# A new order, buffer list and engine list for a fused RWKV-5 and MLP-mixer kernel, with twenty zero products in place of sixteen

## The chip, the core and the metric

The kernel runs on one core of one Trainium2 chip. The metric is the device time of one launch in microseconds (us). Five engines work side by side and wait for one another through semaphores: TensorE (PE in the profile, with its weight loads as PEld), VectorE (DVE), ScalarE (ACT), GpSimd (POOL) and SyncE (SP), which here only issues transfers.

## What is computed

Four sequences of 768 steps and 8 heads of 48 channels go through a linear recurrence with a decaying state, and its output goes through one token-mixing and one channel-mixing MLP with residuals:

```python
for t in range(S):
    cur = np.einsum('bhd,bhe->bhde', u[None] * kt, vt)
    y[:, :, t] = np.einsum('bhd,bhde->bhe', rt, state + cur)
    state = w[None, :, :, None] * state + np.einsum('bhd,bhe->bhde', kt, vt)
...
h = np.maximum(xt @ w_tok1, 0.0) @ w_tok2
u = x + h.transpose(0, 2, 1)
h2 = np.maximum(u @ w_ch1, 0.0) @ w_ch2
return (u + h2)
```

Inputs and output are float32; the products run on bfloat16 copies that accumulate in float32. Nothing of this differs between the two kernels.

## The kernel before

**Tiling.** The recurrence is computed in chunks of 128 steps, six for each of the four batches. In a chunk, k and r are scaled by powers of w (tiles `kr`), turned so that the channels lie on the rows (`tk`, `tr`, `trk` on TensorE, then copied to `ka`, `rka` or `rkb`; from the third batch on by a transposing DMA), multiplied into scores (`at_ps`), masked by VectorE (`AT`), and multiplied with v (`y_ps`). The part that comes from earlier chunks is a product of `rkb` with the state `S`; the state is gathered in a bank `kv_ps` and read out after each chunk. A chunk's own term (u times k times r) is a product of `pr` with `u_blk` (`ad_ps`, then `adg`), multiplied with v by GpSimd (`ydb`) and added into `y_ps`. `y_ps` is read out to `x_b`.

**The first batch** (`pair_unit`, line 823) does two chunks at a time, called window 0, 1 and 2 here: even and odd steps (j = 0, 1) are loaded together (tiles `zr`). For a window TensorE does 8 transposes each of k and r, 32 score products that each use 48 rows and 64 columns of the array, 16 products for `ad_ps`, 16 for `kv_ps` and 32 for `y_ps` that use 64 rows, and some more; an `x N` of the profile often covers half a window. The score products come in two groups of 16 for each window.

**The MLP** of a batch (`mixer`, line 1010) follows when its x is there: `h_ps<-x_b`, `hx_ps` or `hT_ps`, then 12 groups of three `z_ps` products for each half, whose relu is `zr` (written by ScalarE or VectorE), then the `h_ps<-wch,zr` products, the sum to `osb` and the store.

**Order.** Nothing in it is left to a scheduler. `Plan.add` (line 216) collects 886 tasks (890 after the change), each with what it depends on, and `Plan.run` (line 230) emits them in the order of the table `ORDER`. Every engine call goes through `InOrder` (line 273), so each engine's queue has that order, and all rows of the profile name its line 279. `BUFS` gives the buffer number of each tile as it is taken (`m` are the seven PSUM banks), and `ENGINES` says for each task that has a choice which of two engines does it (`flex`, line 223).

**Zero products.** `keep_warm` (line 1191) multiplies a tile of zeros with itself into a bank of PSUM. A wide one is one product of 512 columns; one in quarters is four products of 128 columns each, into the last 128 columns, which the state does not use. `NWARM` is their number and `WIDE_AT` lists the wide ones; a wide one must stand ahead of the first state product of the bank, one in quarters may stand anywhere in the table.

```python
for i in range(512 // cols):
    pe.matmul(bank[0][:, 512 - cols:512], warm[:, 0:128], warm[:, 0:cols], start=fresh or cols == 512, stop=True,
              skip_group_check=True)
```

**Two products with one row.** `w_ps` and `u_ps` (the `spread` function; line 496 for `u_ps`) copy a row of w or u to all partitions: one float32 product of a single row with 384 columns each, which the profile shows as two records.

Of the kernel before, what the change touches and what calls it, by code (L numbers as in the profile page):

```python
# [66 lines left out]
    0, 1, 2, 0, 1, 0, 2, 0, 1, 2, 0, 1, 2, 1, 0, 1, 2, 1, 0, 1, 2, 0, 1, 2,  # L67
],
    'AT1': [
    0, 1, 2, 0, 1, 0, 2, 0, 1, 0, 2, 0, 1, 2, 0, 1, 2, 1, 0, 2, 1, 0, 2, 1,  # L70
# [11 lines left out]
    0, 1, 2, 3, 4, 0, 1, 3, 2, 4, 0, 1, 3, 4, 2, 0, 1, 3,  # L82
# [11 lines left out]
    0, 1, 2, 3, 4, 5, 0, 3, 1, 2, 5, 4, 0, 3, 2, 5, 0, 1, 2, 4, 3, 0, 5, 1, 4, 3, 2,  # L94
# [3 lines left out]
    0, 1, 2, 3, 4, 5, 2, 0, 1, 3, 4, 5, 2, 3, 0, 5, 1, 4,  # L98
],
    'ku': [  # L100
    0, 1, 0, 0, 1, 0, 1, 0, 1, 0, 0, 1,
# [13 lines left out]
],  # L115
    'osb': [
    0, 1, 2, 2, 1, 0, 1, 0, 0, 1, 0, 1, 2, 0, 2, 1, 2, 1, 2, 0, 0, 2, 1, 0, 2,
],
    'pr': [
    0, 1, 1, 0, 1, 0,  # L120
# [5 lines left out]
    0, 1, 2, 3, 0, 1, 2, 3, 1, 0, 3, 2,  # L126
],
    'rka': [
    0, 1, 2, 0, 1, 0,
# [6 lines left out]
    0, 1, 0, 1, 0, 1, 1, 0, 1, 1, 0, 1,  # L136
],
    'rt': [
    0, 1, 2, 3, 4, 0, 2, 3, 1, 0, 4, 2,
# [6 lines left out]
    0, 1, 2, 1, 2, 0, 1, 2,  # L146
],
    'vb': [
    0, 1, 2, 3, 4, 0, 1, 2, 3, 0, 4, 2, 3, 1, 0, 2, 4, 1,
# [5 lines left out]
    0, 1, 2, 3, 4, 5, 0, 2, 1, 3, 4, 0, 5, 1, 2, 3, 4, 0,  # L155
# [5 lines left out]
    0, 1, 2, 1, 0, 2, 0, 1, 2, 0, 2, 1, 2, 1, 0, 1, 2, 1,  # L161
],
    'ydb': [
    0, 1, 2, 0, 1, 0,
# [4 lines left out]
}  # L169
ENGINES = [  # L170
# [9 lines left out]
]  # L180
NWARM = 16
WIDE_AT = [
    0, 1, 2, 3, 4, 5, 6, 7, 8, 9, 10, 11, 12,
]
# [1051 lines left out]
```

## Time and profile before

| what | value |
|---|---|
| median of 3 runs | 165.35 us (165.35 to 165.37) |
| profiled execution | 165.22 us |
| its span (first to last instruction) | 163.3 us |
| PE busy | 158.4 us (97%) |
| DVE / ACT / POOL busy | 119.5 / 66.2 / 79.6 us |
| mean granted TensorE clock | 0.958 |
| DMA | 26.90 MB, 165 GB/s on average |

The profiled execution is 1.9 us longer than its span, and 0.13 us under the median. "Busy" counts the time from a product's start to its modelled end, and products overlap, so busy says little of how much the array does. The profile gives the share of the clock that was granted to TensorE, as PEclk in its slices and in a view that adds up any stretches that one asks for. A row of the timeline reads: start, time, engine, line, operation, names, rows*columns of the array, rows x columns of the moving operand, type, count, and in brackets the idle time before it with what ended it.

### The profile page before, as it was taken

What the parts mean: (1) busy time and instruction counts of PE and PEld (TensorE: products, weight loads), DVE (VectorE), ACT (ScalarE), POOL (GpSimd) and SP (SyncE); (2) the same over time, 40 slices, a digit from 0 to 9 for tenths busy, and PEclk for the clock granted to TensorE, in tenths of its full rate; (3) what the DMA queues carried; (4) which work ended last, traced back from release to release, by engine and by line L of the source; (5) the groups of instructions that cost most, each with busy time, mean ns of one, the idle gap of its engine ahead of it and who ended that gap; (6) DMA issues with size and microseconds to landing.
All of it is one profiled execution on the core that took longest, in us unless ns stands there. A gap on an engine that the chain in (4) does not pass through costs nothing.

```text
span 163.3 us, 4001 instructions
## 1 busy us (share of the span) xinstructions
PE 158.4 (97%) x1593; PEld 106.9 (65%) x1593; DVE 119.5 (73%) x239; ACT 66.2 (41%) x149; POOL 79.6 (49%) x101
## 2 busy tenths in 40 slices
PE   6999999999999999999999999999999999999991
PEld 1486775777676767676667766677667566666671
DVE  6589576576598999889849996998898552782432
ACT  3678285544772263167346524245532014211100
POOL 7279475803908262998995778837622000000000
PEclk9998555999999999999999999999999999999999
DMA  4999979999999679999999799999941055020332
GB/s 127 262 261 253 237 142 235 185 227 174 200 207 203 108 164 174 215 219 167 195 209 218 161 182 195 223 212 193 160 102 52 0 120 139 30 100 0 110 131 96
DMA packets 86821, 26.90 MB, mean 165 GB/s; under 512 B 81554, under 2 KB 85908, under 8 KB 86804
## 3 DMA queue, kind: packets, MB, share of 16 engines
q1 hardware_dynamic: 84448, 23.40, 70.9%
q0 software_dynamic: 2160, 3.15, 11.4%
q8 instruction: 12, 0.20, 0.6%
q10 hardware_dynamic: 196, 0.11, 0.2%
q14 instruction: 5, 0.04, 0.1%
HBM read 20.46 MB, written 4.72 MB: 154 GB/s over the span
## 4 chain that ended last, share of the span: by engine, by line
PE 94%; ACT 2%; DVE 1%; issue 0%
PE h_ps L279 35%; PE z_ps L279 29%; PE kv_ps L279 8%; PE y_ps L279 7%; PE at_ps L279 4%; PE hT_ps L279 3%; PE hx_ps L279 3%; PE tr_ps L279 2%; ACT rkb L279 1%; PE w_ps L279 1%; PE trk L279 1%; PE ad_ps L279 1%; PE tk_ps L279 1%; ACT ka L279 1%; ACT vb L279 1%; DVE pr L279 0%
## 5 line engine op out<-in xcount | busy, mean ns | idle before, releaser
L279 PE MATMUL h_ps<-wch,zr 128*128 128x384 bf16 (+1 forms) x300 | 54.0, 319 | 0.0
L279 PE MATMUL z_ps<-uT,wch 128*128 128x384 bf16 x288 | 52.3, 327 | 0.0
L279 ACT ACTIVATE zr<-z_ps 128x384 bf16<-128x384 f32 x61 | 28.1, 491 | 51.6 <-PE z_ps L279 51.5
L279 PEld LDWEIGHTS <-wch 128*128 128x128 bf16 x288 | 31.7, 114 | 13.5
L279 PEld LDWEIGHTS <-zr 128*128 128x128 bf16 x300 | 27.4, 97 | 15.2
L279 DVE TENSOR_SCALAR zr<-z_ps 128x384 bf16<-128x384 f32 x35 | 18.4, 554 | 14.0 <-PE z_ps L279 13.9
L279 DVE TENSOR_TENSOR AT<-at_ps,mask 128x512 bf16<-128x512 f32 x36 | 23.2, 681 | 3.2 <-PE at_ps L279 3.2
L279 POOL TENSOR_TENSOR yd<-vb,adg 128x384 f32<-128x384 bf16 x13 | 10.7, 830 | 17.8 <-ACT vb L279 5.1
L279 PEld LDWEIGHTS <-kr 128*128 128x128 bf16 (+1 forms) x196 | 13.3, 107 | 3.5 <-issue 1.1
L279 POOL TENSOR_TENSOR kr<-kt,wnat 128x384 bf16<-128x384 f32 x13 | 13.3, 1026 | 1.7 <-DMA kt<-in_k_dram 0.9
L279 POOL TENSOR_TENSOR ku<-kt,u_bc 128x384 f32<-128x384 f32 x11 | 12.0, 1088 | 2.3 <-DMA kt<-in_k_dram 1.6
L279 DVE TENSOR_TENSOR osb<-u_sb,h_ps 128x384 f32<-128x384 bf16 (+1 forms) x16 | 8.4, 525 | 4.9 <-PE h_ps L279 4.8
L279 PEld LDWEIGHTS <-wtok 128*128 128x128 bf16 x78 | 7.3, 100 | 5.2 <-issue 1.3
L279 DVE TENSOR_TENSOR x_b<-y_ps,yd 128x384 bf16<-128x384 f32 x18 | 9.6, 552 | 1.4 <-PE y_ps L279 1.2
L279 DVE TENSOR_TENSOR u_sb<-x_b,hT_ps 128x384 bf16<-128x384 bf16 x15 | 7.5, 549 | 4.0 <-PE hT_ps L279 4.0
L279 PE MATMUL h_ps<-x_b,wtok 128*128 128x384 bf16 x48 | 9.4, 342 | 0.0
L279 POOL TENSOR_TENSOR rku<-ku,rt 128x384 f32<-128x384 f32 x8 | 8.6, 1079 | 1.3 <-DMA rt<-in_r_dram 1.1
L279 POOL TENSOR_TENSOR pr<-rka,rkb 128x512 bf16<-128x512 bf16 x3 | 3.6, 1213 | 11.5 <-DVE rka L279 4.6
L279 PE MATMUL kv_ps<-vb,kr 128*128 128x96 bf16 (+1 forms) x100 | 8.8, 228 | 0.0
L279 PE MATMUL y_ps<-vb,AT 128*128 128x48 bf16 (+1 forms) x240 | 8.8, 191 | 0.0
L279 POOL TENSOR_TENSOR kr<-rt,wp 128x384 bf16<-128x384 f32 x8 | 8.6, 1081 | 0.0
L279 ACT CAST S<-kv_ps 48x192 bf16<-48x192 f32 x20 | 6.3, 313 | 5.2 <-PE kv_ps L279 5.0
(108 smaller groups left out, 211.4 us busy)
## 6 DMA issues: line engine op xcount, KB each, us to landing
out_dram<-osb SPq DMA_DIRECT2D x23, 192.0 KB, 2.2
kt<-in_k_dram SPq DMA_DIRECT2D x18, 192.0 KB, 4.8
vt<-in_v_dram SPq DMA_DIRECT2D x18, 192.0 KB, 4.6
rt<-in_r_dram SPq DMA_DIRECT2D x12, 192.0 KB, 3.7
wch<-in_moe_w_ch_dram POOLq DMA_DIRECT2D x4, 384.0 KB, 6.0
zr<-in_r_dram SPq DMA_DIRECT2D x3, 384.0 KB, 5.1
zr<-in_k_dram SPq DMA_DIRECT2D x3, 384.0 KB, 5.7
zr<-in_v_dram SPq DMA_DIRECT2D x3, 384.0 KB, 9.4
```

What stands on the lines that cost most here:

```text
L279: return lambda *args, **kw: tc.keep_in_program_order(f(*args, **kw))
```

## The change

It writes new tables `ORDER`, `BUFS` and `ENGINES`, and raises the zero products from sixteen to twenty: thirteen wide and three in quarters before, ten wide and ten in quarters after. In columns that is 16 x 512 = 8192 before and 20 x 512 = 10240 after, in 25 and 50 products. All other products, and the code that emits them, are the same; between VectorE, ScalarE and GpSimd some tasks change hands (VectorE 239 instructions to 226, ScalarE 153 to 168, GpSimd 101 to 100).

```diff
 ORDER = [
-    0, 3, 21, 18, 16, 56, 60, 13, 17, 59, 2, 879, 8, 5, 20, 57, 62, 872, 14, 6, 1, 42, 4, 27, 7, 11, 23, 9,
+    0, 3, 22, 17, 18, 56, 60, 20, 16, 57, 59, 49, 873, 46, 1, 62, 881, 8, 4, 2, 871, 13, 5, 7, 27, 25, 14, 21,
...
-NWARM = 16
+NWARM = 20
 WIDE_AT = [
-    0, 1, 2, 3, 4, 5, 6, 7, 8, 9, 10, 11, 12,
+    0, 1, 2, 3, 4, 5, 6, 7, 8, 9,
 ]
```

**TensorE, from the first scores on.** Before, all zero products stand ahead of the first score product. From the last quarter of them on, the queue of TensorE reads (score products 16, `ad_ps` 8, a second group of 16 scores, `kv_ps` 8, then `u_ps`):

```order
L279 LDWEIGHTS warm
L279 MATMUL kv_ps<-warm 128x128
L279 LDWEIGHTS ka
L279 MATMUL at_ps<-rkb,ka 64x128
...
L279 LDWEIGHTS pr_252
L279 MATMUL ad_ps<-u_blk,pr_252 128x8
...
L279 LDWEIGHTS kr_68
L279 MATMUL kv_ps<-vb_240,kr_68 128x96
```

After the change two wide zero products stand between the first 16 scores and `ad_ps`:

```order
L279 LDWEIGHTS ka
L279 MATMUL at_ps<-rkb,ka 64x128
L279 LDWEIGHTS warm
L279 MATMUL kv_ps<-warm 128x512
L279 LDWEIGHTS warm
L279 MATMUL kv_ps<-warm 128x512
L279 LDWEIGHTS pr_253
L279 MATMUL ad_ps<-u_blk,pr_253 128x8
```

The full sequence after the change, from the first scores on, is: 16 scores of window 0, two wide zero products, 8 `ad_ps`, 16 scores, the 8 transposes of r of window 1 (`tr_ps`), `u_ps`, 8 `kv_ps`, one zero product in quarters, 16 scores of window 1, 8 `ad_ps`, the transposes of k of window 2 (`tk_ps`), 8 `kv_ps`, the transposes of r of window 2, then the `y_ps` of window 0. Before, the transposes of r of window 1 stood ahead of all scores, and those of r of window 2 behind the `y_ps` of window 0. Ahead of the first scores there are now eight wide zero products and nine in quarters, where there were thirteen and three.

**VectorE, the same place.** Before (with the tiles' numbers; `zr_127` and `zr_153` are the inputs of windows 1 and 2, `ka` the turned k):

```order
L279 TENSOR_TENSOR kr3_70<-zr_127,wpair_86 128x8x48
L279 CAST u_blk_87<-ud_ps_189 64x4 x2
L279 MEMSET S0_1_94 128x192
L279 COPY ka_228<-tk_ps_210 128x1024
L279 TENSOR_TENSOR pr2_252<-tr_ps_197,ka_228 128x1024
L279 TENSOR_TENSOR kr4_71<-zr_153,u_sb_106 128x8x48
L279 TENSOR_TENSOR AT1_310<-at_ps_261,u_sb_105 128x512
```

After:

```order
L279 CAST iota_77<-iota_i_76 128x8
L279 COPY ka_237<-tk_ps_220 128x1024
L279 TENSOR_TENSOR pr2_253<-tr_ps_209,ka_237 128x1024
L279 CAST u_blk_87<-ud_ps_199 64x4 x2
L279 TENSOR_TENSOR kr1_68<-zr_117,wpair_86 128x8x48
L279 TENSOR_TENSOR kr2_69<-zr_154,u_sb_105 128x8x48
L279 TENSOR_TENSOR AT0_334<-at_ps_303,u_sb_106 128x512
```

The copy of the turned k and the product `pr` of window 0 move ahead of the scaling of r of window 1 (`zr_117` now) and of the casts to `u_blk`.

**SyncE, the first loads.** Before:

```order
L279 DMA zr<-in_r_dram 128x8x96
L279 DMA zr<-in_k_dram 128x8x96 x2
L279 DMA zr<-in_r_dram 128x8x96
L279 DMA zr<-in_v_dram 128x8x96
L279 DMA zr<-in_k_dram 128x8x96
```

After:

```order
L279 DMA zr<-in_r_dram 128x8x96
L279 DMA zr<-in_k_dram 128x8x96 x2
L279 DMA zr<-in_r_dram 128x8x96
L279 DMA zr<-in_k_dram 128x8x96
L279 DMA zr<-in_v_dram 128x8x96
```

The k of window 2 goes one place ahead, past the v of window 0.

More of the change, by code (lines that the diff above doesn't have):

```diff
@@ L66 @@
     'AT0': [
-    0, 1, 2, 0, 1, 0, 2, 0, 1, 2, 0, 1, 2, 1, 0, 1, 2, 1, 0, 1, 2, 0, 1, 2,
+    0, 1, 2, 0, 1, 0, 2, 0, 1, 2, 0, 1, 2, 1, 0, 2, 1, 0, 2, 0, 1, 2, 0, 1,
 ],
     'AT1': [
-    0, 1, 2, 0, 1, 0, 2, 0, 1, 0, 2, 0, 1, 2, 0, 1, 2, 1, 0, 2, 1, 0, 2, 1,
+    0, 1, 2, 0, 1, 0, 2, 0, 1, 2, 0, 1, 2, 0, 1, 2, 0, 1, 2, 0, 1, 2, 0, 1,
 ],
@@ L81 @@
     'adg': [
-    0, 1, 2, 3, 4, 0, 1, 3, 2, 4, 0, 1, 3, 4, 2, 0, 1, 3,
+    0, 1, 2, 3, 4, 1, 2, 0, 3, 4, 1, 2, 4, 0, 2, 3, 1, 4,
 ],
@@ L93 @@
     'kp': [
-    0, 1, 2, 3, 4, 5, 0, 3, 1, 2, 5, 4, 0, 3, 2, 5, 0, 1, 2, 4, 3, 0, 5, 1, 4, 3, 2,
+    0, 3, 4, 1, 2, 5, 0, 1, 3, 5, 4, 2, 0, 3, 1, 5, 4, 2, 0, 3, 1, 2, 0, 4, 3, 1, 5,
 ],
@@ L97 @@
     'kt': [
-    0, 1, 2, 3, 4, 5, 2, 0, 1, 3, 4, 5, 2, 3, 0, 5, 1, 4,
+    0, 1, 2, 3, 4, 5, 0, 1, 3, 2, 5, 4, 0, 1, 2, 5, 4, 3,
 ],
     'ku': [
-    0, 1, 0, 0, 1, 0, 1, 0, 1, 0, 0, 1,
+    0, 1, 1, 0, 1, 0, 0, 1, 0, 1, 0, 1,
 ],
@@ L106 @@
     'm': [
[8 rows of a table removed]
[8 rows of a table added]
 ],
     'osb': [
-    0, 1, 2, 2, 1, 0, 1, 0, 0, 1, 0, 1, 2, 0, 2, 1, 2, 1, 2, 0, 0, 2, 1, 0, 2,
+    0, 1, 2, 1, 1, 0, 1, 0, 1, 0, 1, 1, 1, 2, 0, 2, 1, 1, 0, 1, 2, 0, 2, 0, 1,
 ],
     'pr': [
-    0, 1, 1, 0, 1, 0,
+    0, 1, 1, 1, 0, 1,
 ],
@@ L125 @@
     'rk': [
-    0, 1, 2, 3, 0, 1, 2, 3, 1, 0, 3, 2,
+    0, 1, 2, 3, 1, 0, 2, 3, 0, 1, 3, 2,
 ],
     'rka': [
-    0, 1, 2, 0, 1, 0,
+    0, 1, 2, 0, 0, 1,
 ],
@@ L135 @@
     'rku': [
-    0, 1, 0, 1, 0, 1, 1, 0, 1, 1, 0, 1,
+    0, 1, 0, 1, 0, 1, 0, 1, 1, 0, 1, 0,
 ],
     'rt': [
-    0, 1, 2, 3, 4, 0, 2, 3, 1, 0, 4, 2,
+    0, 1, 2, 3, 4, 0, 2, 1, 3, 4, 0, 1,
 ],
@@ L145 @@
     'u_sb': [
-    0, 1, 2, 1, 2, 0, 1, 2,
+    0, 1, 2, 2, 0, 1, 2, 0,
 ],
     'vb': [
-    0, 1, 2, 3, 4, 0, 1, 2, 3, 0, 4, 2, 3, 1, 0, 2, 4, 1,
+    0, 1, 2, 3, 4, 0, 2, 4, 3, 1, 2, 1, 0, 4, 3, 0, 2, 1,
 ],
@@ L154 @@
     'vt': [
-    0, 1, 2, 3, 4, 5, 0, 2, 1, 3, 4, 0, 5, 1, 2, 3, 4, 0,
+    0, 1, 2, 3, 4, 5, 0, 1, 2, 3, 4, 2, 1, 5, 3, 0, 4, 2,
 ],
@@ L160 @@
     'yd': [
-    0, 1, 2, 1, 0, 2, 0, 1, 2, 0, 2, 1, 2, 1, 0, 1, 2, 1,
+    0, 2, 1, 0, 1, 0, 1, 2, 0, 1, 2, 0, 1, 0, 2, 0, 1, 2,
 ],
     'ydb': [
-    0, 1, 2, 0, 1, 0,
+    0, 1, 2, 0, 0, 1,
 ],
```

116 rows, old and new, of tables (BUFS, ENGINES, ORDER) are left out of this document.

## The prediction

> **What bounds the kernel now.** I read the profile's page first: busy shares and the 40 slices of 4.08 us.
>
> ```profile
> PE 158.4 (97%) x1593; PEld 106.9 (65%) x1593; DVE 119.5 (73%) x239; ACT 66.2 (41%) x149; POOL 79.6 (49%) x101
> ...
> PE   6999999999999999999999999999999999999991
> ...
> PEclk9998555999999999999999999999999999999999
> DMA  4999979999999679999999799999941055020332
> ```
>
> PE never rests between slices 2 and 39, and in slices 5 to 7 it had half its clock. So every PE microsecond saved early can move the end. Next, busy time in stretches of 3.41 us, counted back from the place where the clock falls:
>
> ```profile
> 8.06:11.48 3.42, 3.42 (x46) 2.82 (x45) 3.10 (x9) 2.25 (x6) 2.19 (x3) 1.00 1.28 261
> 11.48:14.89 3.41, 3.11 (x79) 2.03 (x77) 2.94 (x6) 3.16 (x8) 3.25 (x4) 1.00 1.27 261
> 14.89:18.30 3.41, 3.41 (x69) 2.69 (x70) 2.80 (x5) 1.84 (x3) 3.14 (x4) 0.50 1.35 226
> 18.30:21.72 3.42, 3.42 (x51) 2.37 (x53) 1.58 (x4) 1.55 (x4) 0.55 (x1) 0.50 0.92 187
> 21.72:25.13 3.41, 3.41 (x76) 2.56 (x69) 3.03 (x6) 2.17 (x5) 2.62 (x4) 0.50 0.91 195
> 25.13:28.54 3.41, 3.41 (x34) 1.97 (x34) 1.95 (x4) 2.23 (x5) 2.28 (x3) 0.50 1.11 224
> 31.96:160.00 128.04, 127.98 (x1192) 87.40 (x1189) 97.31 (x187) 47.23 (x112) 58.16 (x61) 1.00 0.78 154
> ```
>
> Behind the time stand PE, PEld, DVE, ACT, POOL, then the granted clock and DMA. The clock is 0.50 over exactly 14.89 to 28.54, 13.65 us or four steps of 3.41, and 1.00 from there to the end of the work. From 31.96 to 160.00 PE is idle for 0.06 us. The timeline of PE shows what ran before the fall:
>
> ```profile
> 1.26 1.03 PE L279 MATMUL kv_ps<-warm 128*128 128x512 bf16 x2 [1.26 <-DVE warm L279]
> ...
> 3.80 3.59 PE L279 MATMUL kv_ps<-warm 128*128 128x512 bf16 x11
> 7.32 0.59 PE L279 MATMUL wd_ps<-ident_f,wp 8*128 8x8 f32 x2
> ...
> 9.90 0.60 PE L279 MATMUL kv_ps<-warm 128*128 128x512 bf16 x5
> 10.34 0.61 PE L279 MATMUL tk_ps<-ident,kr 128*128 128x128 bf16 x8
> 10.79 0.61 PE L279 MATMUL tr_ps<-ident,kr 128*128 128x128 bf16 x8
> 11.24 0.39 PE L279 MATMUL kv_ps<-warm 128*128 128x128 bf16 x4
> 11.55 0.42 PE L279 MATMUL at_ps<-rkb,ka 48*64 48x128 bf16 x16
> 11.90 0.35 PE L279 MATMUL ad_ps<-u_blk,pr 128*128 128x8 bf16 x8
> 12.19 0.42 PE L279 MATMUL at_ps<-rkb,ka 48*64 48x128 bf16 x16
> 12.54 0.51 PE L279 MATMUL kv_ps<-vb,kr 64*128 64x96 bf16 x8
> 12.98 0.91 PE L279 MATMUL u_ps<-wp,ones 1*128 1x384 f32 x2
> 14.18 0.36 PE L279 MATMUL ad_ps<-u_blk,pr 128*128 128x8 bf16 x8 [0.30 <-DVE pr L279]
> 14.47 0.42 PE L279 MATMUL at_ps<-rkb,ka 48*64 48x128 bf16 x16
> 14.82 1.00 PE L279 MATMUL tk_ps<-ident,kr 128*128 128x128 bf16 x8
> ```
>
> Start to start, 1024 zero columns take 0.44 us from 9.90 (0.43 ns a column), but 4096 columns take 3.52 us from 3.80 (0.86 ns): half speed there too, up to about 8.06. Now weigh each product by the rows it uses of 128, columns x 0.43 ns. In 11.48 to 14.89: three score groups 3 x 16 x 128 x 0.43 ns x 48/128 = 0.99 us, `kv_ps` 0.17, two `ad_ps` 0.06, `u_ps` next to nothing, the end of a zero product 0.05: 1.27 us or **0.37** of the stretch, and then the clock fell. In 8.06 to 11.48, 32 transposes (four groups from 9.01 to 11.24, the last two shown; 1.76) and zero products (1.2) make **0.87**, and it held. In steps at half clock the same count over the timeline's rows gives shares of 0.78, 0.83 and 0.77 (no rise) and 0.86 (rise at 28.54), and 0.81 from 4.65 to 8.06 (rise). Counting the scores' 64 of 128 columns too turns those into 0.68, 0.73, 0.68 against 0.86 and 0.81; one bar then fits all of them: between 0.73 and 0.81 of half speed, that is **0.37 to 0.40 of full speed**. By columns as well, the stretch that fell had 0.22.
>
> [...]
>
> **The change part by part.** First, does the clock hold at 14.89? I lay the new queue out at these prices. PE starts at 1.26 as before. Two wide zero products and one in quarters, `w_ps`, then four wide and six in quarters, `ud_ps`, and the rest at full speed bring it to the first scores at 11.3 (11.55 before). Behind 11.48 then come: half a score group 0.17, two wide zero products 0.43, `ad_ps` 0.03, scores 0.33, eight transposes 8 x 128 x 0.43 ns = 0.45, `u_ps` 0 (for 0.9 us), `kv_ps` 0.17, quarters 0.22, and half a score group 0.16. Sum 1.96 us or **0.57** by rows, 1.63 or 0.48 with columns: over the bar of 0.37 to 0.40, under the 0.87 that is known to hold. If waits push this by 0.5 us, the last two fall out and the score group comes in whole: 0.51 and 0.42. I take it that the clock holds.
>
> Second, what the half clock cost. These rows give prices on both sides of 28.54:
>
> ```profile
> 16.50 0.64 PE L279 MATMUL at_ps<-rkb,ka 48*64 48x128 bf16 x16
> 17.08 0.50 PE L279 MATMUL y_ps<-S,rkb 128*128 128x96 bf16 x4
> 17.51 0.82 PE L279 MATMUL y_ps<-vb,AT 64*128 64x48 bf16 x32
> 18.27 1.04 PE L279 MATMUL tr_ps<-ident,kr 128*128 128x128 bf16 x8
> ...
> 28.37 0.62 PE L279 MATMUL y_ps<-vb,AT 64*128 64x48 bf16 x32
> 28.92 0.62 PE L279 MATMUL tr_ps<-ident,kr 128*128 128x128 bf16 x8
> 29.48 0.50 PE L279 MATMUL y_ps<-ydb,u_sb 64*128 64x384 bf16 x4
> 29.91 0.82 PE L279 MATMUL h_ps<-x_b,wtok 128*128 128x384 bf16 x4
> ```
>
> From 14.82 to the third window's last `y_ps<-vb,AT` at 28.37 PE needed 13.55 us. At full clock by start-to-start times: transposes 2 x 0.45, scores 3 x 0.35, `kv_ps` 4 x 0.44, `ad_ps` 0.29, 20 products of `rkb` and S (1920 columns, 0.83), two of S and `ident` 0.33, eight of `ydb` 2 x 0.43, four `h_ps` 0.66, two groups with AT at 0.45 (unpriced at full clock; bounds 0.38, half of 0.76, and 0.55, the row at 28.37) = 0.9. Sum 7.6 us. After the change PE meets the same place at 15.4 (0.6 us later: the zero products and transposes moved behind the scores), so PE alone would reach it at **23.0**, and be through at 23.5 instead of 28.92.
>
> Then VectorE is late next. Its timeline:
>
> ```profile
> 12.16 0.56 DVE L279 TENSOR_TENSOR kr<-zr,u_sb 128x384 bf16<-128x384 f32 x1 [0.36 <-DMA zr<-in_k_dram]
> ...
> 16.71 0.56 DVE L279 TENSOR_TENSOR S<-kv_ps,wGm 128x384 bf16<-128x384 f32 x1 [0.20 <-PE kv_ps L279]
> ...
> 19.39 0.69 DVE L279 TENSOR_TENSOR pr<-tr_ps,ka 128x1024 bf16<-128x1024 bf16 x1 [1.51 <-PE tr_ps L279]
> ...
> 21.43 0.18 DVE L279 COPY adg<-ad_ps 128x16 f32<-128x16 f32 x1 [0.74 <-PE ad_ps L279]
> ...
> 23.18 0.56 DVE L279 TENSOR_TENSOR S<-kv_ps,wGm 128x384 bf16<-128x384 f32 x1 [0.38 <-PE kv_ps L279]
> 23.65 1.94 DVE L279 TENSOR_TENSOR AT<-at_ps,u_sb 128x512 bf16<-128x512 f32 x3
> ```
>
> The last mask of the batch ends at 25.59. Waits for PE on the way are 0.20 + 1.51 + 0.74 + 0.38 = 2.83 us; all else is work. With all gone it ends at 22.8, with none gone at 25.6. Two engines that now need each other at nearly the same pace still wait at hand-overs; I keep 1.3 us of it, so the last mask is done at 24.1 and the third window's products at 24.1 + 0.1 + 0.5 = 24.7, against 28.92: **4.2 us** earlier.
>
> Third, the other edits. The four zero products more (0.22 us each at full clock) are in the places above. The earlier load of k for window 2 takes away up to 0.36 us of the wait at 12.16, already inside the hand-overs; its price is the v of window 0 one load later. Tasks that change engines between 31.96 and 160 are under PE's cover (idle 0.06 us), as DVE is busy for 97 of those 128 us; they cost nothing unless one is late, between 0 and the gain itself. The tail behind the last product (160.0 to 163.3) has the same tasks: 0.
>
> Sum: 165.22 - 4.2 = 161.0 on the profiled execution, which lies 0.13 under the median: **161.1 us**. If PE's count alone decided, 28.92 - 23.5 = 5.4 less: 159.8; with no VectorE wait gone, 26.2 and 2.7 less: 162.5.
>
> **The rivals.** *Slower: the clock falls at 14.89 all the same.* Only 0.37 (falls) and 0.87 (holds) are known at full clock, and 0.57 is nearer to the first; the one bar rests on reading half-clock steps as halves. Then PE enters the slow stretch with the scores and `ad_ps` of window 1 still to do, 0.58 + 0.31 at half clock: 0.9 us late, and PE is the bound, so 166.1. The point from which it decides is a bar over 0.57. If the step that rose (25.13 to 28.54, 0.86) is thinned by that shift and misses the rise, one more step of 3.41 us at half clock adds 1.7: 167.8. I price it at 167.
>
> *The clock holds at 14.89 and falls later*, since PE now waits for VectorE. The next two stretches come to 0.70 and 0.64 by rows on my layout, more than 0.57, so it is unlikely; two steps at half clock would give back most: 164.
>
> *The gain is given back later:* the later batches' inputs, relu and stores are asked for 4 us earlier. DMA at 0.78 mean and DVE at 76% speak against it; half given back is 163.
>
> *The stretches lie elsewhere.* The fall lies four steps (13.65) from 1.24, and PE's first product starts at 1.26. If that is chance, say half a step of shift: 13.2 to 16.6 would hold `kv_ps`, quarters, scores, transposes, `kv_ps`, 1.4 us or 0.42, at the bar; a fall at 16.6 leaves 165. [...] Three runs within 0.02 us speak against such a lottery here.
>
> **How the numbers follow.** Forecast 161.1 with 0.47 (own range 159.8 to 162.5); clock falls anyway 0.29 (167); falls later 0.10 (164); given back 0.09 (163); shifted 0.05 (165). Range 159.6 to 167.0: it leaves out the dearer half of the slow case (0.14) and some 0.03 below. Faster by over 0.2% (0.33 us, about what a measurement of this kernel tells from no change): 0.47 + 0.10 + 0.09 = 0.66; within: 0.04, most of the shifted case; slower: 0.30.
>
> **What would show it.** Right: granted clock 1.00 from 8.06 on; the two wide zero products at 11.7 to 12.1; last mask of the batch near 24; the third window's `y_ps<-vb,AT` at 24; PE still idle for less than 1 us up to its end near 156. Wrong: 0.50 in any stretch behind 14.89 (the bar), long waits of PE for `AT` or `S` (VectorE or ScalarE sets the pace), or PE idle in the middle (given back).

## The result, and the profile after

| executions in the first comparison | median | range | n |
|---|---|---|---|
| before | 165.36 us | 165.35 to 165.59 | 4 |
| after | 162.94 us | 162.59 to 167.77 | 4 |

The ratio is 0.9844, 95% interval 0.9813 to 0.9874: faster by 2.4 us, where 4.2 were forecast (161.1); 162.94 lies inside the stated range of 159.6 to 167.0. The ratios in this document leave out executions more than 1.5% above the fastest of their kernel, which here are mostly those that lost the clock, so medians of all executions stand beside them.

The profiled execution of after is the one of 167.77 us, so its trace shows a cost that the other three do not have. From its page, the busy tenths of PE, the granted clock and the DMA share in 40 slices of 4.15 us:

```profile
PE   6999995659999999999999999999999999999991
...
PEclk9999999977999999999999999999999999999999
DMA  4999999999999998199999999999860065111132
```

The 5 5 5 in slices 5 to 7 of before is gone. In its place PE has gaps in slices 7 to 9, and the clock is down for a part of slices 9 and 10, while the DMA engines are busy for 9 tenths or more. The same by stretches, all but the fourth a step of 3.41 us, the length for which the clock fell here, 35.68 to 39.10 (PE, PEld, DVE, ACT, POOL, granted clock, DMA share, GB/s; the DMA share adds up the packets' times and passes 1 in five of the six):

```profile
8.38:11.79 3.41, 3.41 (x58) 2.82 (x58) 2.19 (x7) 2.39 (x4) 1.99 (x3) 1.00 1.28 262
11.79:15.20 3.41, 3.41 (x66) 2.23 (x64) 2.30 (x5) 2.98 (x10) 2.42 (x4) 1.00 1.27 264
15.20:18.62 3.42, 3.42 (x106) 2.77 (x96) 3.42 (x7) 2.50 (x7) 3.42 (x5) 1.00 1.36 220
24.00:28.86 4.86, 2.75 (x54) 1.80 (x53) 3.71 (x3) 1.87 (x4) 2.71 (x3) 1.00 1.15 198
32.27:35.68 3.41, 0.76 (x10) 0.63 (x10) 0.00 (x0) 0.61 (x2) 1.80 (x2) 1.00 0.90 178
35.68:39.10 3.42, 3.42 (x17) 1.79 (x15) 2.58 (x3) 1.66 (x5) 2.10 (x4) 0.50 1.24 235
```

The clock holds behind 15.20: granted 1.00 up to 35.68. The two wide zero products and the third window's last products in the timeline of PE, and then the two places where PE waited for over a microsecond:

```profile
11.73 0.61 PE L279 MATMUL kv_ps<-warm 128*128 128x512 bf16 x2
...
23.90 0.57 PE L279 MATMUL y_ps<-vb,AT 64*128 64x48 bf16 x32
...
26.86 0.33 PE L279 MATMUL kv_ps<-vb,kr 128*128 128x96 bf16 x4 [2.11 <-ACT vb L279]
...
34.92 0.40 PE L279 MATMUL trk<-ident,kr 128*128 128x128 bf16 x4 [3.09 <-POOL kr L279]
```

The third window is through at 24.5 instead of 29.0. The waits behind it are new. What ended them, on ScalarE, GpSimd and VectorE:

```profile
26.29 0.51 ACT L279 CAST vb<-vt 128x384 bf16<-128x384 f32 x1 [3.01 <-DMA vt<-in_v_dram]
```
```profile
24.78 1.95 POOL L279 TENSOR_TENSOR kr<-win,wpair 128x384 bf16<-128x384 f32 x2
33.88 0.99 POOL L279 TENSOR_TENSOR kr<-kt,wnat 128x384 bf16<-128x384 f32 x1 [7.15 <-DMA kt<-in_k_dram]
```
```profile
24.34 2.82 DVE L279 TENSOR_TENSOR kr<-win,wpair 128x384 bf16<-128x384 f32 x1
```

Both inputs belong to the second batch: v of its chunk 0 landed at 26.3, k of its chunk 1 at 33.8. In the wait for the latter PE did 0.76 us of work in a whole step, and the next step ran at half clock. The VectorE row is a scaling that took 0.55 us in the trace of before; here it took 2.82 and ended 0.43 us behind GpSimd's two (26.73), called held below.

### The profile page after: what moved, and what is told of

Same layout as the page of the kernel before. It is cut to its first block, busy times and chain, and to the rows that moved or that the text cites. A ratio compares the mean times of both kernels' runs of the same rounds, so it can differ in the third digit from the quotient of the medians.

```text
span 166.1 us, 4050 instructions
## 1 busy us (share of the span) xinstructions
PE 156.0 (94%) x1618; PEld 106.3 (64%) x1618; DVE 116.8 (70%) x226; ACT 71.3 (43%) x164; POOL 76.0 (46%) x100
## 2 busy tenths in 40 slices
DMA packets 86822, 26.90 MB, mean 162 GB/s; under 512 B 81554, under 2 KB 85908, under 8 KB 86804
## 4 chain that ended last, share of the span: by engine, by line
PE 77%; SPq 11%; DMA 8%; POOL 1%; issue 0%; DVE 0%
PE h_ps L279 33%; PE z_ps L279 29%; SPq L279 11%; DMA kt<-in_k_dram 8%; PE y_ps L279 4%; PE at_ps L279 3%; PE hT_ps L279 3%; PE kv_ps L279 2%; PE hx_ps L279 1%; PE trk L279 1%; PE tr_ps L279 1%; POOL kr L279 1%; PE ad_ps L279 0%; DVE osb L279 0%
## 5 line engine op out<-in xcount | busy, mean ns | idle before, releaser
L279 PE MATMUL z_ps<-uT,wch 128*128 128x384 bf16 x288 | 53.7, 331 | 0.0
L279 ACT ACTIVATE zr<-z_ps 128x384 bf16<-128x384 f32 x67 | 30.6, 492 | 46.1 <-PE z_ps L279 45.8
L279 PEld LDWEIGHTS <-zr 128*128 128x128 bf16 x300 | 27.4, 98 | 15.4
L279 DVE TENSOR_SCALAR zr<-z_ps 128x384 bf16<-128x384 f32 x29 | 15.2, 554 | 8.9 <-PE z_ps L279 8.9
L279 POOL TENSOR_TENSOR yd<-vb,adg 128x384 f32<-128x384 bf16 x16 | 13.2, 829 | 15.7 <-DVE adg L279 8.4
L279 POOL TENSOR_TENSOR kr<-kt,wnat 128x384 bf16<-128x384 f32 x14 | 14.5, 1042 | 8.0 <-DMA kt<-in_k_dram 7.7
L279 PEld LDWEIGHTS <-kr 128*128 128x128 bf16 (+1 forms) x196 | 11.8, 97 | 8.7 <-POOL kr L279 3.4
L279 POOL TENSOR_TENSOR rku<-ku,rt 128x384 f32<-128x384 f32 x10 | 10.5, 1052 | 7.5 <-DVE ku L279 7.4
L279 ACT CAST vb<-vt 128x384 bf16<-128x384 f32 x16 | 7.9, 512 | 9.9 <-DMA vt<-in_v_dram 7.8
L279 PE MATMUL kv_ps<-vb,kr 128*128 128x96 bf16 (+1 forms) x100 | 7.5, 205 | 2.1 <-ACT vb L279 2.1
L279 PE MATMUL kv_ps<-warm 128*128 128x128 bf16 (+1 forms) x50 | 7.9, 321 | 1.3 <-DVE warm L279 1.3
```

The lines of the kernel that those rows point to most:

```text
L279: return lambda *args, **kw: tc.keep_in_program_order(f(*args, **kw))
```

## The experiments

`ORDER` is edited in one line: a pair (n, a) takes task n out and puts it behind task a. "Share" is counted by rows and columns of the array: columns of the product x 0.833 ns at half clock (in the trace of before, products of 384 columns start 320 ns apart from 26.63 on, and wide zero products 427 ns apart ahead of 8.06) or half of that, 0.417, at full clock (products of 384 columns start 162 to 163 ns apart there), x rows/128 x columns of the array/128, of a step of 3.41 us. The 0.43 ns that the prediction gives for full clock would make the shares 3% larger.

**The changed kernel once more, unaltered.** 

> The changed kernel once more, unaltered, for a trace of its usual execution. Both theories: 162.6 us, granted clock 1.00 from about 8 us on. Theory A (the order of the second batch's first loads, set anew by the change, starves TensorE): TensorE idles some 4 to 5 us between 24 and 36 us, waiting for the copy of v of chunk 0 and for the scaled k of chunk 1, both of which wait for their loads. Theory B (the 16 DMA engines are full up to 34 us, and no order of loads helps) expects the same waits here, and parts from A in the kernel with the loads reordered.

On a second chip: 162.79 us median of 10 (162.24 to 167.6) against 163.62 of 19 executions of before (161.12 to 165.35); ratio 0.9984 (0.9937 to 1.003). Its profiled execution took 162.8 us. Clock up at 10.05 instead of 8.38, so the steps of 3.41 us lie elsewhere in this execution (its phase, below), no fall before 160, and one wait of PE over 0.3 us:

```profile
28.49 0.81 PE L279 MATMUL h_ps<-x_b,wtok 128*128 128x384 bf16 x4 [1.35 <-DVE x_b L279]
```

k of chunk 1 landed at 29.0 there: the same input moved by almost 5 us between two executions of one program. The sum closes: the third window ends at 25.28 instead of 28.99, 3.7 us earlier, the wait takes 1.35 of it back, and 2.4 are left, which is what lies between this execution and the 165.22 of before. But before isn't the kernel that the first comparison showed: it spreads over 4 us here, and no difference is shown.

**Before, once more, with a profile.** 

> Nothing is changed: this is the kernel before. Theory E (the clock's step grid starts anywhere, so the low stretch between 11 and 15 us of this kernel loses the clock in some executions only, and the profiled execution of 165.4 us was of the expensive kind): the executions spread from 161 to 165.5 us, and their mean granted clock tells how many half-clock steps each had; a trace whose rise is elsewhere than at 8.06 has a smaller fall or none, and in it the third window's last y_ps<-vb,AT ends near 25 instead of 28.92, with the second batch's waits then as in the changed kernel (2 to 4 us of PE waits between 25 and 36). Rival F (the grid is tied to the program's start): every execution takes 165.4 within 0.3, rise at 8.06.

163.68 us median of 10 (162.39 to 165.07). The profiled execution took 163.11 us. The clock was up from 6.49 and did not fall until the end. Its steps over the place of the fall, then the end of the third window and PE's later waits:

```profile
9.90:13.31 3.41, 3.14 (x69) 2.32 (x66) 2.76 (x5) 2.88 (x7) 3.39 (x4) 1.00 1.27 261
13.31:16.73 3.42, 3.08 (x94) 2.21 (x92) 3.42 (x6) 2.89 (x8) 3.28 (x5) 1.00 1.33 242
```
```profile
23.96 0.57 PE L279 MATMUL y_ps<-vb,AT 64*128 64x48 bf16 x32
...
31.36 0.68 PE L279 MATMUL z_ps<-uT,wch 128*128 128x384 bf16 x3 [0.86 <-DMA wch<-in_moe_w_ch_dram]
...
34.10 0.40 PE L279 MATMUL tr_ps<-ident,kr 128*128 128x128 bf16 x4 [0.39 <-POOL kr L279]
35.06 0.40 PE L279 MATMUL tr_ps<-ident,kr 128*128 128x128 bf16 x4 [0.56 <-POOL kr L279]
```

This is the most telling run. With the steps at 9.90 and 13.31 the low stretch is cut so that each part has a share of 0.40 and 0.41, where the step from 11.48 had 0.22. The third window ends at 24.53, as early as in the changed kernel, but the execution is only 2.1 us shorter than the 165.22. So of 4.46 us saved in front, 2.35 were given back, and part of that is seen: waits of 0.86, 0.39 and 0.56 us between 30 and 36, where the execution with the fall had none. The rival (a grid tied to the program's start) is out.

All 103 executions of before in these experiments, by mean granted clock: at 0.996 or more 45, median 163.3 us; 0.988 to 0.989 (about one step lost) 8, 164.0; 0.968 to 0.979 (two or three) 32, 164.0; 0.954 to 0.958 (four) 18, 165.2. The 14 of after: at 0.996 or more 10, median 162.7; 0.987 to 0.990 4, median 167.4. The means are 163.9 and 163.9, the medians 163.8 and 162.8. The best of before took 161.1; eight of its executions, all at full clock, lie below the best of after, 162.24.

**Three zero products of after taken to the front.** The two wide ones at 11.7 and a later one in quarters:

```diff
+(872, 157), (877, 872), (882, 877)
```

> The changed kernel with its three late zero products (two wide, one in quarters) moved ahead of the first scores: as many zero products, none in the stretch with few rows. If the clock goes by rows and columns used, the stretch from about 11.6 to 15.1 us falls from 0.54 to about 0.35 and the clock is halved from about 15 us for three or four steps of 3.41 us: 166 to 168 us. If the transposes moved into that stretch are enough by themselves, it stays at 162.6 us.

167.98 us median of 4 (165.5 to 171.13); ratio 1.0225 (1.0079 to 1.0371). The step that fell had a share of 0.376:

```profile
13.41:16.83 3.42, 3.22 (x70) 2.22 (x67) 2.05 (x5) 3.12 (x10) 3.30 (x4) 1.00 1.33 239
16.83:20.24 3.41, 3.41 (x73) 2.86 (x70) 3.41 (x6) 2.38 (x5) 1.81 (x3) 0.50 1.28 244
```

That cost one step. Two more were lost behind a wait of 3.24 us for `x_b`, where the step from 27.07 had 0.29: VectorE's held scaling took 4.69 us there. So not all of the 5 us are the price of the low stretch.

**The same three left in place and at their length, on 1 row.**

```diff
-pe.matmul(bank[0][:, 512 - cols:512], warm[:, 0:128], warm[:, 0:cols], ...
+pe.matmul(bank[0][:, 512 - cols:512], warm[0:rows, 0:128], warm[0:rows, 0:cols], ...
-t = add("PE", "warm", keep_warm(512 if i in WIDE_AT else 128), [t_warm])
+t = add("PE", "warm", keep_warm(512 if i in WIDE_AT else 128, 1 if i in (1, 6, 11) else 128), [t_warm])
```

> The changed kernel, with the three zero products whose removal was tried (tasks 872, 877 and 882) left in their places and at their lengths, but using 1 row of the array instead of 128: they take the same time and the output is the same. Theory G (the clock weighs a product by the rows that it uses): they weigh a 128th, so the clock is as without them; steps between 13 and 21 us have shares of 0.37 to 0.48 by rows and columns and some fall, the mean granted clock of most executions is 0.95 to 0.99, and the median is 165 us or more. Theory H (the clock looks at the time in which products run, and the rows are nothing to it): no fall there in any execution, mean clocks of 0.996 to 1.0 in most, and a median of 162.5 to 163, as the changed kernel.

167.29 us median of 6 (165.51 to 171.0), mean clocks 0.946 to 0.987; ratio 1.0212 (1.0134 to 1.0291). The profiled execution (170.9) has the clock up at 7.47:

```profile
11.38 0.60 PE L279 MATMUL kv_ps<-warm 1*128 1x512 bf16 x2
```
```profile
10.88:14.29 3.41, 3.41 (x62) 2.11 (x62) 2.51 (x6) 2.86 (x9) 2.44 (x3) 1.00 1.29 264
14.29:17.71 3.42, 3.42 (x51) 2.60 (x49) 3.13 (x6) 2.57 (x7) 3.42 (x5) 0.50 1.34 224
...
24.53:27.95 3.42, 3.42 (x52) 1.99 (x50) 2.57 (x5) 1.05 (x4) 1.51 (x3) 0.50 0.99 171
27.95:31.36 3.41, 3.23 (x62) 2.17 (x61) 3.41 (x3) 1.63 (x4) 3.39 (x5) 1.00 1.21 208
```

PE was busy in 3.41 of the 3.41 us from 10.88, and the clock fell for four steps (a fifth was lost at 34.77, behind a wait of 3.80 us for `x_b`). The two products take 0.60 us as with 128 rows (0.61), so the time on PE does not tell the two steps apart. By the share this one has 0.28, and the run below with two of the later edits, with the clock up at the same 7.47 and 128 rows, had 0.40 in that very step and held:

```profile
10.88:14.29 3.41, 3.41 (x63) 2.22 (x63) 2.36 (x7) 3.13 (x9) 2.41 (x3) 1.00 1.30 265
14.29:17.71 3.42, 3.42 (x106) 2.86 (x104) 3.42 (x7) 2.85 (x8) 3.42 (x5) 1.00 1.34 218
```

That is the premise of the change, as these two steps show it.

**Before with three of its zero products behind the first scores.**

```diff
+(871, 144), (880, 871), (886, 147)
```

> The kernel before with nothing but three of its sixteen zero products moved behind the first scores (two wide, one in quarters behind the first state products): its own order, buffers and engines otherwise. Share of the low stretch 0.37 to about 0.5, so the clock should hold. Theory A: this order asks for k of chunk 1 at 13.5 us and for the MLP weights at 23 to 28 us, so little is starved, and the full clock is worth 3 to 4.5 us: 161 to 162.3 us, at or under the changed kernel. Theory B: the same bytes have to land by the same work, so TensorE waits as in the changed kernel: 162.6 to 163.5 us. If the clock falls all the same: 165.4 us.

163.56 us median of 10 (161.82 to 165.24); ratio 1.0062 (1.0 to 1.0124). No fall at the low stretch in the trace (0.40 there), but a wait later, and the step around it fell:

```profile
27.45 1.44 PE L279 MATMUL h_ps<-x_b,wtok 128*128 128x384 bf16 x4 [1.99 <-DVE x_b L279]
```
```profile
23.97:27.38 3.41, 1.49 (x44) 1.05 (x45) 1.66 (x3) 2.36 (x4) 2.47 (x5) 1.00 1.22 245
27.38:30.79 3.41, 3.34 (x16) 1.96 (x16) 1.72 (x6) 0.16 (x1) 1.95 (x2) 0.50 1.18 203
```

By its median nothing is gained over before (163.62). Two of its ten executions were at a clock of 0.975 and 0.976 and one at 0.954. None of the three was traced, so whether they lost it at the low stretch or at the later wait is not shown.

**After, with v of chunk 0 and k of chunk 1 asked ahead of r of chunks 2 and 3.**

```diff
+(70, 68), (69, 70), (71, 69), (74, 71)
```

> The changed kernel with SyncE asking for the second batch's v of chunk 0, r of chunks 0 and 1 and k of chunk 1 straight behind k of chunk 0, ahead of r of chunks 2 and 3. Theory A: the waits for v of chunk 0 (2.1 us) and for k of chunk 1 (3.1 us) shrink to under 1 us each: 160 to 161 us. Theory B: r of chunks 2 and 3 and the weights come later by as much, and TensorE waits for them instead: 162 to 163 us.

170.66 us median of 4 (167.83 to 170.89). The two waits went, and a longer one came: VectorE stood at the scaling of r of chunks 2 and 3, with the cast that PE needs queued behind it.

```profile
33.70 0.56 DVE L279 TENSOR_TENSOR kr<-win,wpair 128x384 bf16<-128x384 f32 x1 [9.54 <-DMA win<-in_r_dram]
34.17 0.55 DVE L279 CAST x_b<-y_ps 128x384 bf16<-128x384 f32 x1
```
```profile
34.78 1.44 PE L279 MATMUL h_ps<-x_b,wtok 128*128 128x384 bf16 x4 [8.70 <-DVE x_b L279]
```

**After, with both first channel weights asked later** (behind the scalings of r of chunks 0 and 1):

```diff
+(121, 313), (122, 121)
```

> The changed kernel with the two loads of the first channel weights (wch 0 and 1, GpSimd's queue) asked for behind the scaling of r of chunk 0, some 4 us later. Theory C: what is left over after the clock holds is a race of loads; in the slow executions k of chunk 1, asked for at 20.5 to 21.9 us, lands behind these weights at 33.8 us, in the usual ones ahead of them at 29.0 us, and TensorE waits 3 us. With the weights later it always lands by about 26 us: no execution over 164 us, the usual one at 162.0 to 162.8 us. Theory B (full DMA engines): what is moved behind is waited for instead, `z_ps` waits for wch, 163 us or more.

164.83 us median of 10 (162.91 to 167.04); ratio 1.0111 (1.0046 to 1.0177). k of chunk 1 is in time; v of chunk 0 isn't, and the step around that wait loses the clock (0.26):

```profile
27.04 0.33 PE L279 MATMUL kv_ps<-vb,kr 128*128 128x96 bf16 x4 [2.22 <-ACT vb L279]
```

**After, with VectorE's scaling of r of chunks 2 and 3 behind the `x_b` cast** (and its buffer number moved with it):

```diff
+(345, 313)
```

> The changed kernel with VectorE's scaling of r of chunk 2 one place later, behind the last cast to x_b of the first batch. Theory D: that scaling took 2.8 us in place of 0.55 because it could not run beside GpSimd's scalings of r of chunk 0 (1.96 us), and the cast behind it, which TensorE waits for (1.35 us), came 2.3 us late. Then the usual execution falls by 1 to 1.5 us, to 161.2 to 161.8 us, and the wait of h_ps for x_b is gone; the slow executions stay. If the 2.8 us are a wait for the load instead, the cast does not come earlier by more than 0.5 us and the time stays at 162.6 us.

166.25 us median of 11 (162.65 to 167.8): five at 162.65 to 163.14 and six at 166.25 to 167.8; ratio 1.0028 (0.9952 to 1.0104). The better five gain nothing over the changed kernel's 162.7, where 1 to 1.5 us were expected. In the profiled execution the scaling took 1.30 us and PE waited for nothing behind it, but k of chunk 1 was late again:

```profile
33.90 0.61 PE L279 MATMUL trk<-ident,kr 128*128 128x128 bf16 x4 [4.07 <-POOL kr L279]
```

**The last two edits together.** 

> Both edits together. Theories C and D: the usual execution at 160.8 to 161.6 us and none over 163 us, so faster than the changed kernel in its median by 1 to 2 us. Theory B: no better than 162.6 us.

164.31 us median of 6 (163.23 to 165.07); ratio 1.0104 (1.0027 to 1.018). This is the run with 0.40 at 10.88. PE's wait is again the one for v of chunk 0, 2.37 us, and a step with a share of 0.20 falls.

**All three edits together.** 

> All three repairs together: VectorE's scaling behind the x_b casts, both first channel weights asked behind the second batch's first scalings, and v of chunk 0 and k of chunk 1 asked ahead of r of chunks 2 and 3. Theories C and D (each wait has a cause of its own and each repair takes one away): no PE wait above 1 us between 24 and 36, 161 to 161.5. Theory B (the bytes asked before 30 us set the end of the stretch, and a repair only moves the wait to another input): a wait of 2 us or more remains at some input, or later at the weights, 162.6 or more.

164.97 us median of 12 (163.56 to 167.23); ratio 1.0107 (1.0062 to 1.0153). v and k are in time; r of chunks 2 and 3 landed at 28.3, the scaling was then held (3.02 us) beside GpSimd's, and with it the relu behind it:

```profile
28.29 3.02 DVE L279 TENSOR_TENSOR kr<-win,wpair 128x384 bf16<-128x384 f32 x1 [2.15 <-DMA win<-in_r_dram]
31.24 0.55 DVE L279 TENSOR_SCALAR h1r<-h_ps 128x384 bf16<-128x384 f32 x1
```
```profile
31.84 1.46 PE L279 MATMUL hx_ps<-wtok,h1r 128*128 128x384 bf16 x4 [3.55 <-DVE h1r L279]
```

**After, without the loads of the first channel weights.** They become two memsets to zero early on GpSimd, so the first channel product is left out in effect:

```diff
+(121, 19), (122, 121)
-sent[i] = pool.dma_start(t, src.rearrange(how, p=128))
+sent[i] = pool.memset(t, 0.0) if i in (2, 3) else pool.dma_start(t, src.rearrange(how, p=128))
```

> The two loads of the first channel weights (the third and fourth weight transfers on GpSimd's queue) are replaced by two memsets to zero in GpSimd's idle stretch of 5 to 9 us: the part of the output behind the first channel product is left out, all products keep their sizes. Theory B (the transfers are full until about 34 us, and what the second batch's inputs wait for is the bytes of the weights asked among them): the waits of 2 to 4 us for v of chunk 0, k of chunk 1 and r of chunk 2 go, only VectorE's scaling beside GpSimd remains, no step is lost between 24 and 36, all executions take 159.5 to 161.5. Rival A (the order of asking, or the queue of SP, sets when these inputs land, whatever else moves): k of chunk 1 still lands after 29 and PE still waits 2 us or more there, 162.5 to 165.

162.03 us median of 10 (160.63 to 165.07); ratio 0.9909 (0.9862 to 0.9956), beside 164.05 of 29 executions of before on the same chip. k of chunk 1 landed at 27.6 and no step fell. v of chunk 0 was still late; it is asked ahead of where those weights were, so they may not be what holds it:

```profile
26.70 0.33 PE L279 MATMUL kv_ps<-vb,kr 128*128 128x96 bf16 x4 [1.94 <-ACT vb L279]
```

Taking bytes away gave a lower median than the changed kernel's, which no reordering did. The gain is about 0.8 us, less than expected, with that wait left, and the two intervals against before overlap (0.9862 to 0.9956 and 0.9937 to 1.003). And k of chunk 1 was no earlier than with the same weights only asked later (27.5 and 27.2 in the two profiled executions).

The traces together say more. In eight of them SyncE asks for k of chunk 1 at 20.3 to 20.7. Where GpSimd asked for no more weights until 22.9 or later (the two runs that take the three zero products out of the stretch or put them on 1 row) it landed at 25.0 and 25.1. With the second token weights asked at 20.2 to 20.6 and the channel weights later or never (three runs) it landed at 27.2 to 27.6. With the first channel weights asked by 22.0 as well (three runs) it landed at 29.0 to 33.8, and the earlier these weights were asked, the later k was: for 21.16, 21.42 and 21.97 it landed at 33.8, 32.8 and 29.0. The first and the last of these are the two executions of the unaltered changed kernel:

```profile
21.16 0.75 POOL L279 DMA_DIRECT2D wch<-in_moe_w_ch_dram  x1
```
```profile
21.97 0.76 POOL L279 DMA_DIRECT2D wch<-in_moe_w_ch_dram  x1
```

**The reordered loads, with all that waits for r of chunks 2 and 3 put behind seven channel products** (and the buffer numbers moved with it).

```diff
+(345, 237), (346, 345), (347, 264), (348, 347), (70, 68), (69, 70), (71, 69), (74, 71)
```

> The changed kernel with v of chunk 0 and k of chunk 1 asked ahead of r of chunks 2 and 3, as in the run that reordered the loads, and with everything that waits for r of chunks 2 and 3 (its two scalings, its transposes and their copy) put behind the first batch's casts and seven of its channel products instead of ahead of them; the weights stay where they are. Theory C (each wait has its own cause, and each late input can be put behind work that is there): the wait of 8.7 us of the reordered loads goes, PE waits less than 1.5 us in all between 24 and 36, no half-clock step there, executions of 160.5 to 161.8. Theory B (the bytes asked before 30 us set the pace of this stretch, whatever the order): 2 us or more of PE waits remain, at the channel weights or at r of chunks 2 and 3, and the median is 162.5 or more.

167.32 us median of 6 (167.03 to 168.16); ratio 1.0203 (1.0152 to 1.0254). PE worked without a wait from 21 to 34.7, later than in any other run of the changed kernel's variants, and then ran dry:

```profile
30.19:33.60 3.41, 3.35 (x25) 2.21 (x23) 0.24 (x1) 3.41 (x9) 0.00 (x0) 1.00 1.13 204
33.60:37.01 3.41, 1.13 (x7) 0.56 (x5) 2.19 (x3) 1.65 (x4) 1.44 (x2) 1.00 0.91 203
37.01:40.43 3.42, 1.84 (x11) 1.09 (x12) 1.90 (x4) 0.00 (x0) 2.16 (x3) 0.50 0.91 175
```
```profile
34.78 0.56 DVE L279 TENSOR_TENSOR kr<-kt,wnat 128x384 bf16<-128x384 f32 x1 [4.35 <-DMA kt<-in_k_dram]
```

Now k of chunk 2 is the late one, with relus and the other scaling queued behind it on VectorE. Each order tried picked another input to be late, and no version that computes everything beat the changed kernel's 162.7. That the bytes asked before 30 us set the pace, whatever the order, fits this but is not shown: the kernel before moves the same 26.90 MB in another order, and its best executions took 161.1.

## Why the prediction was right, and where it was not

**The number: right in direction and range, and in part by luck.** The 165.4 of before is what it costs when four steps fall. By their clocks 18 of 103 later executions had that; by its times the first comparison met it in each of its four.

**The clock holds: right.** Forecast shares of 0.57 by rows and 0.48 with columns in the stretch behind 11.48; in the profiled execution 0.54 and 0.44 in 11.79 to 15.20, held. None of the nine traces of after and of its variants with all zero products in place fell there; both without their weight fell. The margin is thin: at other phases the share of that step was 0.376 to 0.38 in three of the nine, at the bar, where the prediction allowed for 0.42.

**The bar by rows and columns: right.** It was put at 0.37 to 0.40 of full speed. At full clock the highest falls in these traces are at 0.28, 0.29, 0.30 and 0.376, and the lowest holds at 0.376, 0.38, 0.40 and 0.41. At half clock there is no rise at 0.73 and a rise at 0.74, half of which is 0.37. No step of the fourteen traces up to 158 us is out of this order, so in them the bar lies at 0.37 to 0.38. By rows alone nothing orders the half-clock steps: 0.83 gave no rise, 0.78 did. Nor does the order hold with the transposes left out of the count: then steps at 0.18 and 0.21 held and one at 0.28 fell. The half-clock shares of the prediction are at 0.833 ns a column, not at twice the 0.43 that it gives.

**The third window at 24.2 to 24.7 instead of 28.92: the number right**, 23.9 to 24.47, **but not the engine that set it.** The forecast had VectorE set the pace, with the last mask at 24.1 and PE's own work through at 23.0. The last mask was done at 23.38, half a us ahead of its use, and PE waited 0.21 us once in that stretch:

```profile
21.49 1.89 DVE L279 TENSOR_TENSOR AT<-at_ps,u_sb 128x512 bf16<-128x512 f32 x3
```

PE's own work was summed too low, 7.6 us from 15.4 where it took 8.4 from 15.52 (the 20 products of `rkb` and S took 1.15 instead of 0.83). That the two misses left the number right is luck.

**The step that failed is the sum.** It took the 4.2 us straight through to the end ("165.22 - 4.2"), because PE is idle for 0.06 us behind 31.96 in before. That cover was made by the fall: PE was late, so what the second batch needs was in time. With PE 4.5 us earlier, and the DMA engines full, it waits for v of chunk 0, k of chunk 1 or VectorE's held scaling: 2.11 and 3.09 us in the profiled execution of after, 1.35 in the other. The rival "given back later" (0.09, half of the gain, 163) is what happened, and it spoke of a DMA share of 0.78, the mean over 128 us, where the stretch that matters has 0.90 to 1.24. The giving back is not of this change's making alone: before without its fall gave back 2.35 us too, at other waits.

**The argument for a fixed step grid failed.** Three runs within 0.02 us and a grid that passed 1.24, near PE's first product at 1.26, were a coincidence of phase. PE's first product started at 1.26 in every trace, and the clock rose anywhere from 6.49 (before, once more) to 10.05 (after, once more). The prediction weighed a shift of the steps at 0.05, as a way to lose; it decided what before costs (a median of 163.3 us at a mean clock of 0.996 or more, of 165.2 at 0.954 to 0.958). The change takes most of that lottery away (no fall in the low stretch in nine traces, though three were at the bar), and enters another: a wait of 3 us for k of chunk 1 with a half-clock step behind it, which its first profiled execution met and, by their times and clocks, three others of 14. Averaged over the 103 and the 14 executions, which are not from the same chips throughout, the two kernels are equal (163.9); the first comparison caught before at its worst phase in each execution, and why it did so every time is open. That k of chunk 1 landed at 29.0 in one execution and at 33.8 in another goes with when GpSimd asked for the channel weights (21.97 and 21.16), and that with the phase of the clock (up at 10.05 and 8.38); three traces in one order do not prove the link.

## What to carry to other kernels

Before you credit a time saved early to the end, ask whether what PE will need next is there by then: a stretch without waits behind a slow one may be made by the slowness. A few runs that agree closely can share a phase that other executions don't have (165.35 to 165.59 us in four here, 161.1 to 166.25 in 103 later), so look at the spread and at each execution's mean clock. Fill a low stretch with products that use the whole array (here a step held at a share of 0.40 with them on 128 rows and fell at 0.28 with them on 1), and check at several places of the step grid.

## What the runs showed of the hardware

- What put the falls of these fourteen traces in order is the share by rows x columns of the array, not the time in which PE is busy: behind a step of 3.41 us with PE busy for all of it and a share of 0.28 (two zero products on 1 row) the granted clock was 0.50; with the same two products on 128 rows, in another run at the same phase, the step had 0.40 and the clock behind it was 1.00.
- VectorE's scaling took longer where scalings of GpSimd ran beside it: 2.82 us in after, 3.02 in the run with all three edits and 4.69 in the one with the zero products at the front, instead of 0.55 to 0.56 in before and in the run with the loads reordered, and it ended 0.42 to 0.43 us behind the last of GpSimd's. In two other runs (first channel weights asked later; without them) it came in between GpSimd's two and took 1.35, and those two took 2.58 instead of 1.95. Which of them goes first does not follow from the starts in the trace: in after VectorE's record starts at 24.34, GpSimd's two at 24.78, and VectorE's ended behind both, 27.16 against 26.73.
- When an input asked on SP's queue landed went with the weights asked on GpSimd's: k of chunk 1, asked at 20.3 to 20.7 in eight traces, landed at 25.0 to 25.1, 27.2 to 27.6 or 29.0 to 33.8 as none, one or two weight transfers were asked between 20.2 and 22.0. With 1.2 MB of weights left out (26.90 MB moved in all, then 25.72) it landed at 27.6.
